# Attention, gated FFN and a mixture of experts in one kernel: the norm's weight beside the root, Newton on VectorE, masks zeroed by VectorE, a new order

## Chip, cores and metric

One Trainium2 chip; the kernel runs on one of its cores. The metric is device microseconds (us) of one execution, lower is better. Engines: PE is TensorE (matmuls), PEld its weight loads, DVE is VectorE, ACT ScalarE, POOL GpSimd, SP SyncE (it issues DMAs).

## What is computed

Three stages, one after the other, all float32. The heads of the attention's output lie side by side, so that 4 x 576 tokens of 8 x 64 features become x, 2304 x 512.

```python
# attention: batch 4, heads 8, seq 576, head_dim 64, window 64
scores = q @ k.T / 8 ; keep 0 <= i - j < 64 ; softmax ; @ v
# FFN: w_gate, w_val 512 x 1536, w_out 1536 x 512
rms = sqrt(mean(x*x, -1) + 1e-6);  xn = x / rms * rms_g
x = (silu(xn @ w_gate) * (xn @ w_val)) @ w_out
# experts: 8, w1 512 x 1024, w2 1024 x 512
e = argmax(x @ w_gate);  gate_w = softmax(...)[e];  eom = sigmoid(x @ w_output_gate)[e]
out = gate_w * eom * (relu(x @ w1[e]) @ w2[e])
```

## The kernel before

**Precision.** Nearly every matmul is run on pairs: an operand is rounded to fp32r ("hi", a cast, helper `hi_i`, L348 on ACT, L350 on POOL, L352 on DVE) and the rest is kept as a second fp32r ("lo", a subtraction, `lo_i`, L355). Three matmuls (hi hi, hi lo, lo hi) make a product. So each operand costs a cast and a subtraction, and ACT, DVE and POOL are kept busy beside PE. `times` is a TENSOR_TENSOR multiply (L358).

**Attention.** 18 tiles of 128 tokens. For the tiles below K["qzt"] the queries lie in a buffer q_all that is padded with zeros (`zeros`, L557), and the scores are 128x128 matmuls (L672 to L674) with the mask added by a matmul of `masks` against the identity (L661) for the first tiles. Later tiles run scores as 64-row matmuls on halves of the array (L700, called tiled here), 12 for a half tile, and add the mask on DVE. Then row maximum (L726, DVE), exponent (L730, ACT), reciprocal (L742), division (L747 on ACT, L358 on POOL or DVE), transposition (L763) and the product with the values into a bank, from where x is copied.

**Norm.** For each tile: squares, a matmul that sums them, mean (L869), a seed for 1/sqrt (L874, an exponent on the bits), two Newton steps on a column of 128 numbers (`newton`: ten chained operations, on POOL), a transposition on PE that spreads the root (L900), and `norm` (L906): four DVE instructions, each x times rms_g times root for 128 features. Then hi and lo of xn.

**FFN.** 12 chunks f of 128 hidden features, for groups of tiles: GROUPS puts units 0 and 1 (tiles 0 to 3) into group 0. L1050 to L1052 are the gate and value matmuls, L1062 to L1075 the activation, L1092 to L1094 the product with w_out. The FFN's weights arrive as 64-bit floats and are converted during group 0 (`conv`): c1 and c0 on ACT (L948, L953), then bit operations on DVE (L958, L969), then hi and lo. Chunks below K["lact"] take c0 on ACT, the rest a DVE operation in its place.

**Experts.** Tokens are routed, scattered to slots in HBM by indirect DMA, and worked through in blocks of up to 512 tokens: a "first" block during the last FFN group, a narrow block of 128 (L1547 to L1559), then wide ones (L1588 to L1590, L1622 to L1624). Results go out by an indirect DMA that POOL issues (`put`, L1640); each put waits until the one before it has landed. Weights are split into hi (cast) and lo (subtraction) as they come.

**What sets the order.** `Plan.order` is a list scheduler in Python that runs when the kernel is built. Each `pl.op` names the engines that may do it with a cost in us for each, buffers read and written, and a priority; the scheduler simulates five engines, a lock for operations of DVE and POOL ("pv"), buffers and DMAs, and writes every engine's instructions in the order that the simulation gives. K holds its tuned numbers. While PE has nothing ready near the start, it gets filler matmuls (L505), until K["warm"] us of the simulated time. So a changed cost moves instructions everywhere.

Of the kernel before, what the change touches and what calls it, by code (L numbers as in the profile page):

```python
# [32 lines left out]
HOP = 0.2  # L33
TICK, FULL = 3.4133, 1.275
HOPS = {"t": 0.0, "a": 0.12, "v": 0.12, "p": 0.12, "s": 0.0}
K = dict(
    qzt=6, spe=4, lact=12, warm=50, wf=1.17, flead=37.337, pvt=5, nwv=0, port=1, t0=44.466, pp=93.644,
    lead=1.877, clead=14.32, stag=6.769, stage=1.089, slack=0.045, mpe=5, nt=2, look=-0.002, marg=0.239, dw=2.625, ewl=20.108,
    ews=5.63, xld=30.179, xtn=3.067, mlead=8, vb=0.61, vb2=0.298, tb=124.917, share=-0.071, rlead=4.252, span=0.82, wl=3.695,
# [17 lines left out]
class Op:  # L57
    __slots__ = ("engs", "fn", "prio", "seq", "succ", "need", "deps", "bufs", "eng", "start", "end", "dma", "done", "dur", "rows", "lock")
# [9 lines left out]
class Plan:  # L68
# [10 lines left out]
    def op(self, engs, fn, r=(), w=(), hold=(), prio=0.0, dma=0.0, after=(), rows=1.0, lock="p"):  # L79
        o = Op()  # L80
        o.engs, o.fn, o.prio, o.seq, o.dma, o.rows = engs, fn, prio, len(self.ops), dma, rows
        o.lock = lock
# [33 lines left out]
    def order(self):  # L116
# [11 lines left out]
        def enable(o):  # L128
            for e in o.engs:
                t = max((d.end + (HOPS[e] if d.eng == e and not d.dma else HOP) for d in o.deps), default=0.0)  # L130
                heapq.heappush(wait, (t, o.seq, e, o))
# [6 lines left out]
        ticks = {}  # L138

# [29 lines left out]
        while left:  # L169
# [5 lines left out]
            for e in free:  # L175
# [3 lines left out]
                while ready[e]:  # L179
                    it = heapq.heappop(ready[e])  # L180
# [33 lines left out]
                    if e == "t":  # L214
                        c = pe_time(now, c, o.rows)
# [13 lines left out]
                    for b in o.bufs:  # L229
                        b.left -= 1  # L230
                        b.end = max(b.end, o.end)
                        if not b.left:
                            b.slot["buf"], b.slot["free"] = None, b.end + HOP
# [37 lines left out]
def attention_ffn_moe(  # L271
# [102 lines left out]
    def cost(n, kind):  # L374
        f = n / 512.0
        return {
            "hs": {"a": 0.12 + 0.48 * f, "p": 0.1 + 0.52 * f, "v": 0.09 + 0.29 * f},
            "ls": {"v": 0.09 + 0.555 * f, "p": 0.17 + 1.12 * f},
            "hp": {"a": 0.1 + 0.48 * f, "v": 0.08 + 0.56 * f},
            "lp": {"v": 0.08 + 0.56 * f},  # L380
        }[kind]
# [20 lines left out]
    def c_ident(e):  # L402
        t = ident.t
        nc.gpsimd.memset(t, 0.0)
# [4 lines left out]
    def c_masks(e):  # L409


        nc.gpsimd.memset(masks.t, 0.0)
# [24 lines left out]
    pl.op({"p": 0.4}, c_ident, w=[ident], prio=-100)  # L437
    pl.op({"p": 2.5}, c_masks, w=[masks], prio=-99)
# [115 lines left out]
    def zeros(e):  # L554
        for j in range(2):
            a = qz[64 * j:64 * j + 64, :, :, :, 64 - 64 * j:P - 64 * j].rearrange("p z i c t -> p (z i c) t")
            nc.gpsimd.memset(a.bitcast(F32), 0.0)  # L557

    if K["qzt"]:
        pl.op({"p": 1.9}, zeros, w=[(qb, "zeros")], prio=-99.5)  # L560

    def attention_front(t):
# [13 lines left out]
        if t < K["qzt"]:  # L576
            for j in range(2):
# [3 lines left out]
                def turned(j=j):  # L581
# [7 lines left out]
                    {"v": 0.6}, lambda e, own=own, turned=turned: scaled_lo(e, own(1), turned(), own(0)),  # L589
                    r=[rq, (qb, (j, 0))], w=[(qb, (j, 1))], prio=pr, lock="pv",  # L590
                )
        else:
# [4 lines left out]
                {"v": 0.6}, lambda e: scaled_lo(e, qb.t[:, 1], view(rq), qb.t[:, 0]), r=[rq, (qb, 0)], w=[(qb, 1)],  # L597
# [4 lines left out]
        if t == 0:  # L602
# [4 lines left out]
            pl.op({"v": 0.55, "p": 0.7}, kz, w=[(kt, "p")], prio=pr)  # L607
# [19 lines left out]
    def attention_tile(t, kt, rv):  # L627
# [8 lines left out]
        if t == 0:  # L636
            of = val[-1] = Buf("val")
            pl.op(
                {"p": 0.9, "v": 1.07},
# [7 lines left out]
            {"v": 0.62, "a": 0.97, "p": 1.1}, lambda e: hi_i(e, of.t[0:64], al.t[0:64]), r=[al], w=[of], prio=pv_, lock="pv"  # L647
# [3 lines left out]
        for hf in range(2):  # L651
# [3 lines left out]
            if zt:  # L655
                bk = bank()

                def mmz(e, bk=bk, hf=hf):
# [18 lines left out]
                    {"t": 1.36 + 0.2 * pm}, mmz, r=[qb, kt] + ([ident_b, masks] if pm else []), w=[bk], hold=[s],  # L677
# [13 lines left out]
            if not zt:  # L691
# [13 lines left out]
                pl.op({"t": 1.0}, mm, r=[qb, kt], w=bks, hold=[s], prio=ps_, rows=0.75)  # L705
                for j, bk in enumerate(bks):
# [12 lines left out]
                    pl.op({"v": 0.67}, mask, r=[bk, masks], w=[(s, j)], prio=ps_)  # L719
# [31 lines left out]
            pl.op({"v": 0.64}, mx, r=[sc or s], w=[mb], prio=ps_)  # L751
            pl.op({"a": 1.5}, ex, r=[sc or s, mb], w=[s, mb], prio=ps_)
            pl.op({"v": 0.15, "a": 0.17}, guard, r=[mb], w=[mb], prio=ps_)
            pl.op({"v": 0.15}, rc, r=[mb], w=[mb], prio=ps_)
            pl.op({"p": 1.08, "v": 0.64, "a": 1.2}, nm, r=[s, mb], w=[s], prio=ps_, lock="pv")
# [23 lines left out]
        for hf in range(2):  # L779
            px_ = pr + (4 + hf) * sg  # L780
            if t < K["pvt"]:
# [16 lines left out]
                for r in range(2):  # L798
# [4 lines left out]
                    pl.op({"a": 0.34, "v": 0.36}, ev3, r=[bk], w=[(x, (hf, r))], prio=px_)  # L803
                continue
            for r in range(2):
# [40 lines left out]
        pl.op({"a": 0.6, "v": 0.64, "p": 1.28}, sqr, r=[x], w=[sq], prio=pn_, lock="pv")  # L846
# [12 lines left out]
        if t >= K["spe"]:  # L859
            n = 1  # L860
            pl.op({"p": 1.21, "v": 0.66}, add, r=[sq], w=[sq], prio=pn_, lock="pv")
# [16 lines left out]
        def newton(e):  # L878
            ms, yy, a, b = (y.t[:, z:z + 1] for z in range(4))
            ne = ve[e]  # L880
            times(e, a, yy, yy)
            times(e, a, a, ms)
            ne.tensor_scalar(out=a, in0=a, scalar1=-0.5, scalar2=1.5, op0=ALU.mult, op1=ALU.add)
            times(e, yy, yy, a)
            times(e, a, yy, yy)
            times(e, a, a, ms)
            ne.tensor_scalar(out=b, in0=a, scalar1=0.375, scalar2=-1.25, op0=ALU.mult, op1=ALU.add)
            times(e, b, b, a)
            ne.tensor_scalar(out=b, in0=b, scalar1=1.875, scalar2=None, op0=ALU.add)
            times(e, yy, yy, b)  # L890

        pl.op({"a": 0.14, "v": 0.12}, mean, r=[bk], w=[y], prio=pn_)
        pl.op({"a": 0.25}, seed, r=[y, seed_b], w=[y], prio=pn_)
        pl.op({"p": 3.6, "v": 1.9} if t < K["nwv"] else {"p": 3.6}, newton, r=[y], w=[y], prio=pn_, lock="")
# [16 lines left out]
        pl.op({"v": 1.15}, norm, r=[x, bk2, g_sb], w=[x], prio=pn_)  # L911
# [13 lines left out]
    def conv(kind, f):  # L925
# [112 lines left out]
    def ffn_step(p, f, n, new, acc, pr):  # L1038
# [7 lines left out]
        def gv(e, w, bk, which):  # L1046
# [53 lines left out]
    def ffn_end(p, acc, pr):  # L1100
        for j in range(SIZES[p]):
# [13 lines left out]
            pl.op({"a": 0.58, "v": 0.64}, ev, r=[acc[j]], w=[(x2[p, j], 0)], prio=pr + 1)  # L1115
# [33 lines left out]
    def route(p):  # L1149
# [4 lines left out]
        for j in range(PT):  # L1154
# [21 lines left out]
            pl.op({"a": 0.6, "v": 0.65}, r2, r=[bk], w=[bx], prio=pr)  # L1176
# [33 lines left out]
        def rf(e):  # L1210
# [9 lines left out]
            {"v": 1.41}, rb, r=[g["lm"], iota_m] + ([rt_b["pf"][(p - 1) % 2]] if p else []),  # L1220
# [594 lines left out]
```

## Time and profile before

| what | value |
|---|---|
| median of 3 runs | 883.3 us (882.4 to 884.68) |
| the profiled execution | 887.55 us, span 885.5 us |
| PE busy | 855.3 us, 97% of the span, 5786 matmuls |
| DVE, ACT, POOL busy | 548.3, 400.5, 298.9 us |
| mean granted PE clock | 0.981 |

The span is the profiled part of the execution; 2.05 us lie outside of it. The profile gives busy time by engine, groups of instructions, waits (an engine's idle time and the instruction that ended it) and a timeline. PEclk is the clock that PE was granted, as a share of 2.4 GHz; 0.50 is the lower level, 1.2 GHz. A busy PE at that level does half as much.

### The profile page before, as it was taken

To read this page: it belongs to the slowest core of one execution; us is meant where nothing else is said; L and a number is where in the kernel's file an instruction comes from. 1 tells how busy PE (TensorE), PEld (TensorE's weight loads), DVE (VectorE), ACT (ScalarE), POOL (GpSimd) and SP (SyncE) were. 2 spreads that over 40 slices of the span, in tenths; PEclk is the share of its full clock that TensorE was granted. 3 is DMA by queue.
4 is the path that set the end of the run, shared out by engine and by line. 5 is a ranking of instruction groups with operands and counts; after the bars stand their busy time and mean duration, and the time that the engine had idled before them with its cause. 6 is when DMAs were issued, how large, how long until landed. Compare 5 with 4: busy or idle time off the path is not lost. (4 is left out here: it accounts for less than half of the span.)

```text
span 885.5 us, 16016 instructions
## 1 busy us (share of the span) xinstructions
PE 855.3 (97%) x5786; PEld 780.3 (88%) x5786; DVE 548.3 (62%) x1258; ACT 400.5 (45%) x1050; POOL 298.9 (34%) x510
## 2 busy tenths in 40 slices
PE   8989999999999999999999999999989999999995
PEld 8978998999899999889998999999968888989984
DVE  6887898977775673756466553554576253556640
ACT  7888776664643452445342342222333132343420
POOL 6886543315324231443224220210133132233320
PEclk8998999999999999999999999999998999999998
DMA  6266799637524431265014317540095344656500
GB/s 195 92 246 219 245 277 316 236 120 253 188 80 140 174 131 38 96 201 172 8 67 160 143 49 285 171 175 1 27 321 206 119 144 147 210 176 228 192 25 19
DMA packets 54016, 139.28 MB, mean 157 GB/s; under 512 B 6800, under 2 KB 6800, under 8 KB 53936
## 3 DMA queue, kind: packets, MB, share of 16 engines
q1 hardware_dynamic: 50912, 128.40, 42.9%
q0 software_dynamic: 3024, 9.85, 2.9%
q8 instruction: 46, 0.75, 0.4%
q14 instruction: 34, 0.28, 0.1%
HBM read 113.69 MB, written 24.54 MB: 156 GB/s over the span
## 5 line engine op out<-in xcount | busy, mean ns | idle before, releaser
L1050 PE MATMUL bank<-xn,w 128*128 128x384 f32 (+1 forms) x672 | 216.6, 322 | 3.3 <-POOL xn L350 2.3
L1051 PE MATMUL bank<-xn,w 128*128 128x384 f32 (+1 forms) x672 | 211.4, 315 | 0.6 <-DVE xn L355 0.6
L1052 PE MATMUL bank<-xn,w 128*128 128x384 f32 (+1 forms) x672 | 211.6, 315 | 0.2 <-DVE w L355 0.2
L1050 PEld LDWEIGHTS bank<-xn,w 128*128 128x128 f32 x672 | 128.1, 191 | 8.2 <-POOL xn L350 2.5
L1051 PEld LDWEIGHTS bank<-xn,w 128*128 128x128 f32 x672 | 128.2, 191 | 2.9 <-DVE xn L355 0.8
L1052 PEld LDWEIGHTS bank<-xn,w 128*128 128x128 f32 x672 | 128.0, 190 | 0.4 <-DVE w L355 0.4
L355 DVE TENSOR_TENSOR w<-raw,w 128x512 fp32r<-128x512 f32 x114 | 85.3, 790 | 10.7 <-POOL w L350 5.7
L1092 PE MATMUL bank<-wo,h 128*128 128x512 f32 x216 | 87.4, 405 | 1.3 <-POOL h L350 1.1
L1094 PE MATMUL bank<-wo,h 128*128 128x512 f32 x216 | 85.2, 394 | 0.0
L1093 PE MATMUL bank<-wo,h 128*128 128x512 f32 x216 | 85.0, 394 | 0.0
L1075 DVE TENSOR_TENSOR u<-u,bank 128x384 f32<-128x384 f32 (+1 forms) x84 | 41.5, 494 | 69.1 <-PE bank L1052 67.1
L1062 ACT ACTIVATE u<-bank 128x384 f32<-128x384 f32 (+1 forms) x84 | 37.2, 443 | 84.2 <-PE bank L1052 74.8
L350 POOL TENSOR_SCALAR w<-raw 128x512 fp32r<-128x512 f32 x59 | 36.3, 631 | 107.0 <-PE bank L1052 39.1
L1622 PE MATMUL bank<-w,eh 128*128 128x512 f32 (+1 forms) x168 | 67.9, 404 | 3.4 <-DVE eh L355 3.4
L1588 PE MATMUL bank<-xT,w 128*128 128x256 f32 (+4 forms) x224 | 68.5, 306 | 0.3 <-DVE eh L1599 0.3
L348 ACT CAST h<-u 128x384 fp32r<-128x384 f32 (+1 forms) x68 | 31.9, 470 | 80.2 <-DVE u L1075 74.1
L1590 PE MATMUL bank<-xT,w 128*128 128x256 f32 (+4 forms) x224 | 68.2, 304 | 0.0
L1589 PE MATMUL bank<-xT,w 128*128 128x256 f32 (+4 forms) x224 | 68.1, 304 | 0.0
L1067 DVE SCALAR_TENSOR_TENSOR u<-u,bank 128x384 f32<-128x384 f32 (+1 forms) x84 | 41.4, 493 | 42.1 <-ACT u L1062 41.5
L1624 PE MATMUL bank<-w,eh 128*128 128x512 f32 (+1 forms) x168 | 67.2, 400 | 0.0
L1623 PE MATMUL bank<-w,eh 128*128 128x512 f32 (+1 forms) x168 | 67.1, 400 | 0.0
L348 ACT CAST w<-raw 128x512 fp32r<-128x512 f32 x67 | 38.9, 618 | 35.1 <-PE bank L1052 17.4
(262 smaller groups left out, 1856.3 us busy)
## 6 DMA issues: line engine op xcount, KB each, us to landing
w<-whd SPq DMA_DIRECT2D x80, 512.0 KB, 3.8
raw<-in_moe_w_dram SPq DMA_DIRECT2D x64, 512.0 KB, 4.6
whd<-w SPq DMA_DIRECT2D x24, 512.0 KB, 5.1
raw<-in_moe_w_gate_dram SPq DMA_DIRECT2D x12, 512.0 KB, 5.4
raw<-in_moe_w_val_dram SPq DMA_DIRECT2D x12, 512.0 KB, 4.3
raw<-in_moe_w_out_dram SPq DMA_DIRECT2D x12, 512.0 KB
rx<-in_q_dram SPq DMA_DIRECT2D x18, 256.0 KB, 3.1
rx<-in_k_dram SPq DMA_DIRECT2D x18, 256.0 KB, 2.8
```

Of the source, the lines that this page charges most:

```text
L348: nc.scalar.copy(o, i)
L355: ve[e].tensor_tensor(out=o, in0=i, in1=h, op=ALU.subtract)
L1050: nc.tensor.matmul(o, lhsT=h_, rhs=xn.t[:, 0, kk], start=(kk == 0), stop=False)
L1051: nc.tensor.matmul(o, lhsT=h_, rhs=xn.t[:, 1, kk], start=False, stop=False)
L1052: nc.tensor.matmul(o, lhsT=l_, rhs=xn.t[:, 0, kk], start=False, stop=(kk == KD - 1))
L1092: nc.tensor.matmul(o, lhsT=h.t[:, 0, c], rhs=wo.t[:, 0, f], start=(n == 0), stop=False)
L1093: nc.tensor.matmul(o, lhsT=h.t[:, 0, c], rhs=wo.t[:, 1, f], start=False, stop=False)
L1094: nc.tensor.matmul(o, lhsT=h.t[:, 1, c], rhs=wo.t[:, 0, f], start=False, stop=(n == NF - 1))
L1588: nc.tensor.matmul(o, lhsT=wh, rhs=x.t[:, 0, kk, 0:N], start=(kk == 0), stop=False)
L1589: nc.tensor.matmul(o, lhsT=wh, rhs=x.t[:, 1, kk, 0:N], start=False, stop=False)
L1590: nc.tensor.matmul(o, lhsT=wl, rhs=x.t[:, 0, kk, 0:N], start=False, stop=(kk == KD - 1))
L1622: nc.tensor.matmul(bk.t[0:M], lhsT=hh, rhs=wh, start=(f == 0), stop=False)
```

## The change

- `masks` and `ident` are zeroed by DVE (`c_zero`); POOL only runs the selects on them. The zeros of q_all are two operations that either engine may take.
- A new operation `weigh` multiplies x by rms_g between the squares and the norm. `norm` becomes a single DVE instruction over 512 features.
- `newton` takes 8 instructions on DVE (10 on POOL, as before). It may go to either; the order gives 17 of 18 tiles to DVE. `weigh` went to ACT (four instructions) for all but one tile, which POOL has.
- Tiled scores of both halves of a tile get the same priority, and the scheduler charges 0.165 us for each change between tiled and other matmuls. K["qzt"] 7: tile 6 now has padded scores.
- K["lact"] 8: for the chunks from 8 on, c0 is replaced by a DVE operation.
- Costs of nearly all operations, a latency for each engine in place of one for all, and K are new, so the order is new. Instructions in the whole program: POOL 533 to 318, DVE 1286 to 1399, ACT 929 to 1036. Casts of the experts' weights: DVE 2 to 49, POOL 59 to 8; their subtractions on POOL 14 to 34. Fillers 182 to 250.

```diff
-HOP = 0.2
+SW = 0.165
-HOPS = {"t": 0.0, "a": 0.12, "v": 0.12, "p": 0.12, "s": 0.0}
+LAT = {"t": 0.17, "a": 0.15, "v": 0.15, "p": 0.12, "s": 0.2}
-    qzt=6, spe=4, lact=12, warm=50, wf=1.17, flead=37.337, pvt=5, nwv=0, port=1, t0=44.466, pp=93.644,
+    qzt=7, spe=4, lact=8, warm=60, wf=1.17, flead=36.084, pvt=5, nwv=1, port=1, t0=50.832, pp=94.912,
...
-        nc.gpsimd.memset(t, 0.0)
...
-        nc.gpsimd.memset(masks.t, 0.0)
...
+    def c_zero(e):
+        nc.vector.memset(ident.t, 0.0)
+        nc.vector.memset(masks.t, 0.0)
...
-                pl.op({"t": 1.0}, mm, r=[qb, kt], w=bks, hold=[s], prio=ps_, rows=0.75)
+                pl.op({"t": 0.67}, mm, r=[qb, kt], w=bks, hold=[s], prio=pr + 2 * sg + hf * K["hfs"], rows=0.75, tiled=True)
...
+        def weigh(e):
+            if e == "a":
+                for kk in range(KD):
+                    nc.scalar.activation(out=x.t[:, kk], in_=x.t[:, kk], func=AF.Copy, scale=g_sb.t[:, kk:kk + 1])
+            else:
+                both(e, x.t, x.t, g_sb.t.unsqueeze(2).to_broadcast([P, KD, P]), ALU.mult)
+
+        pl.op({"a": 1.05, "p": 1.3, "v": 0.64}, weigh, r=[x, g_sb], w=[x], prio=pn_ + 0.05, lock="pv")
...
-            times(e, a, yy, yy)
-            times(e, a, a, ms)
-            ne.tensor_scalar(out=a, in0=a, scalar1=-0.5, scalar2=1.5, op0=ALU.mult, op1=ALU.add)
-            times(e, yy, yy, a)
-            times(e, a, yy, yy)
-            times(e, a, a, ms)
-            ne.tensor_scalar(out=b, in0=a, scalar1=0.375, scalar2=-1.25, op0=ALU.mult, op1=ALU.add)
-            times(e, b, b, a)
-            ne.tensor_scalar(out=b, in0=b, scalar1=1.875, scalar2=None, op0=ALU.add)
-            times(e, yy, yy, b)
...
+            for c1, c0 in ((-0.5, 1.5), (0.375, -1.25)):
+                if e == "v":
+                    ne.scalar_tensor_tensor(out=a, in0=yy, scalar=yy, in1=ms, op0=ALU.mult, op1=ALU.mult)
+                else:
+                    times(e, a, yy, yy)
+                    times(e, a, a, ms)
+                ne.tensor_scalar(out=b, in0=a, scalar1=c1, scalar2=c0, op0=ALU.mult, op1=ALU.add)
+                if c1 > 0:
+                    times(e, b, b, a)
+                    ne.tensor_scalar(out=b, in0=b, scalar1=1.875, scalar2=None, op0=ALU.add)
+                times(e, yy, yy, b)
...
-        pl.op({"p": 3.6, "v": 1.9} if t < K["nwv"] else {"p": 3.6}, newton, r=[y], w=[y], prio=pn_, lock="")
+        pl.op({"v": 1.5} if t < K["nwv"] else {"p": 2.95, "v": 1.5}, newton, r=[y], w=[y], prio=pn_, lock="pv")
...
-            for kk in range(KD):
-                nc.vector.scalar_tensor_tensor(
-                    out=x.t[:, kk], in0=x.t[:, kk], scalar=g_sb.t[:, kk:kk + 1], in1=bk2.t[:, 0:P],
-                    op0=ALU.mult, op1=ALU.mult,
-                )
...
+            both("v", x.t, x.t, bk2.t[:, 0:P].unsqueeze(1).to_broadcast([P, KD, P]), ALU.mult)
```

**POOL at the start, before.** POOL's instructions up to the first select on the masks (an AFFINE_SELECT writes the value outside of a triangle):

```order
L404 MEMSET ident 128x128
L405 ISA
L405 AFFINE_SELECT ident<-ident 128x128
L557 MEMSET q_all 64x16x64 x2
L412 MEMSET masks 128x512
L416 AFFINE_SELECT masks<-masks 64x2x64
```

After the change, the same stretch of POOL:

```order
L569 MEMSET q_all 64x16x64
L414 ISA
L414 AFFINE_SELECT ident<-ident 128x128
L424 AFFINE_SELECT masks<-masks 64x2x64
L428 AFFINE_SELECT masks<-masks 64x2x64
```

One half of the zeros of q_all and the zeros of `ident` and `masks` left POOL; on DVE they are its first instructions and its seventh.

**Tile 3's root and norm, before.** POOL, from the Newton steps (y is the column with mean and root) to the cast of xn:

```order
L358 TENSOR_TENSOR y_1190<-y_1190 128x1 x2
L883 TENSOR_SCALAR y_1190<-y_1190 128x1
L358 TENSOR_TENSOR y_1190<-y_1190 128x1 x3
L887 TENSOR_SCALAR y_1190<-y_1190 128x1
L358 TENSOR_TENSOR y_1190<-y_1190 128x1
L889 TENSOR_SCALAR y_1190<-y_1190 128x1
L358 TENSOR_TENSOR y_1190<-y_1190 128x1
L350 TENSOR_SCALAR wo<-t_1219 128x512
L367 TENSOR_SCALAR q_all<-rx_839 64x8x64
L350 TENSOR_SCALAR xn<-x_1071 128x4x128
```

After the change, DVE for the same tile (L368 is `times`, and the norm where a bank is read; L977 and L988 convert weights):

```order
L905 SCALAR_TENSOR_TENSOR y_1262<-y_1262 128x1
L909 TENSOR_SCALAR y_1262<-y_1262 128x1
L368 TENSOR_TENSOR y_1262<-y_1262 128x1
...
L912 TENSOR_SCALAR y_1262<-y_1262 128x1
L368 TENSOR_TENSOR y_1262<-y_1262 128x1
L977 SCALAR_TENSOR_TENSOR t_1320<-t2k_1319,t_1320 128x512
L368 TENSOR_TENSOR x_1044<-x_1044,bank_1347 128x512
L988 SCALAR_TENSOR_TENSOR t_1320<-raw_1161,t_1320 128x512
L365 TENSOR_TENSOR xn<-x_1044,xn 128x4x128
```

The chain stands on DVE, with one weight operation between it and the norm, which is one row, and one between the norm and the lo of xn.

**The narrow expert block, before.** DVE around the lo of eh, the hidden layer of the narrow block (w are weights of the next expert):

```order
L355 TENSOR_TENSOR xT_8276<-bank_8297,xT_8276 128x4x64
L355 TENSOR_TENSOR w_8335<-raw_8230,w_8335 128x512
L355 TENSOR_TENSOR w_8337<-raw_8239,w_8337 128x512
L355 TENSOR_TENSOR w_8335<-raw_8230,w_8335 128x512
L355 TENSOR_TENSOR eh_8346<-bank_8345,eh_8346 128x512
```

After the change:

```order
L1532 COPY meta_3_154<-xs_8347 64x1
L362 CAST w_8390<-raw_8352 128x512 x2
L365 TENSOR_TENSOR eh_8376<-bank_8375,eh_8376 128x512
L365 TENSOR_TENSOR xT_8317<-bank_8382,xT_8317 128x4x128
L365 TENSOR_TENSOR eh_8393<-bank_8392,eh_8393 128x512
```

Three subtractions that need POOL's casts stood ahead of eh's lo; now two casts of DVE's own do, and the subtractions of that weight are POOL's.

## Rows read from the trace of the kernel before

**Rows 1.** Stretches: length; PE, PEld, DVE, ACT, POOL busy; PEclk, DMA, GB/s.

```profile
60.00:80.00 20.00, 16.04 (x106) 14.41 (x106) 18.73 (x35) 17.65 (x51) 12.88 (x19) 0.83 0.70 245
...
100.00:180.00 80.00, 78.27 (x586) 72.38 (x586) 73.96 (x139) 58.32 (x140) 31.34 (x38) 1.00 0.83 270
...
640.00:672.00 32.00, 26.99 (x118) 21.14 (x117) 22.54 (x63) 9.95 (x19) 9.40 (x13) 0.89 0.86 300
672.00:868.00 196.00, 195.68 (x1132) 172.48 (x1131) 100.24 (x189) 66.23 (x133) 61.05 (x74) 1.00 0.44 152
```

**Rows 2.** PE's waits: line and releaser, us in total, times, longest.

```profile
PE bank L900 <- POOL y L358: 3.5, 4, 1.5
PE bank L1622 <- DVE eh L355: 3.4, 1, 3.4
PE bank L1050 <- POOL xn L350: 2.3, 1, 2.3
PE bank L661 <- POOL masks L423: 2.1, 1, 2.1
```

**Rows 3.** A shorter stretch at the start, columns as in rows 1.

```profile
10.00:15.00 5.00, 5.00 (x32) 4.91 (x32) 2.69 (x7) 3.01 (x14) 1.47 (x3) 0.50 0.48 184
```

**Rows 4.** Timeline at the start, POOL: start, us, instruction.

```profile
1.32 1.94 POOL L557 MEMSET q_all<- 64x1024 f32 x2
3.32 0.53 POOL L412 MEMSET masks<- 128x512 bf16 x1
```

**Rows 5.** The same for PE.

```profile
8.11 0.38 PE L661 MATMUL bank<-masks,ident_b 128*128 128x512 bf16 x1 [2.08 <-POOL masks L423]
...
8.38 0.28 PE L673 MATMUL bank<-kt,q_all 128*128 128x128 f32 x1
8.49 0.30 PE L674 MATMUL bank<-kt,q_all 128*128 128x128 f32 x1
```

**Rows 6.** Timeline of POOL in tile 1's Newton steps.

```profile
43.25 1.25 POOL L358 TENSOR_TENSOR y<-y 128x1 f32<-128x1 f32 x2
...
48.23 0.19 POOL L358 TENSOR_TENSOR y<-y 128x1 f32<-128x1 f32 x1
```

**Rows 7.** Groups of DVE, 0 to 200 us: busy, mean ns, idle before.

```profile
L906 DVE SCALAR_TENSOR_TENSOR x<-x,g_sb,bank 128x128 f32<-128x128 f32 x24 | 6.7, 342 | 4.1 <-PE bank L900 4.1
...
L739 DVE TENSOR_SCALAR m<-m 128x4 f32<-128x4 f32 x4 | 2.5, 617 | 1.2 <-ACT s L730 1.2
...
L358 DVE TENSOR_TENSOR s<-s,m 128x512 f32<-128x512 f32 x2 | 1.4, 684 | 0.0
```

**Rows 8.** Timeline of DVE in the routing: chained small operations.

```profile
632.81 0.18 DVE L1184 TENSOR_TENSOR lm<-lg,mx 128x24 f32<-128x24 f32 x1
633.02 0.18 DVE L1188 SCALAR_TENSOR_TENSOR cd<-lm,iota_m 128x24 f32<-128x24 f32 x1
```

**Rows 9.** A group of ACT, whole span.

```profile
L747 ACT ACTIVATE s<-s,m 128x128 f32<-128x128 f32 x36 | 11.4, 393 | 0.6 <-DVE m L742 0.4
```

**Rows 10.** Timeline of PE around tiled scores.

```profile
152.83 0.91 PE L700 MATMUL bank<-kt,q_all 64*128 64x192 f32 x12
153.68 0.50 PE L1092 MATMUL bank<-wo,h 128*128 128x512 f32 x1
...
253.79 1.58 PE L700 MATMUL bank<-kt,q_all 64*128 64x192 f32 x24
255.31 0.44 PE L1050 MATMUL bank<-xn,w 128*128 128x384 f32 x1
```

**Rows 11.** Timeline of POOL, DVE and PE around the narrow expert block.

```profile
657.93 0.97 POOL L1640 DMA_INDIRECT out_dram<-osb,meta  x1 [8.02 <-ACT osb L1553]
...
659.60 4.53 DVE L355 TENSOR_TENSOR w<-raw,w 128x512 fp32r<-128x512 f32 x3 [4.11 <-POOL w L350]
664.05 0.68 DVE L355 TENSOR_TENSOR eh<-bank,eh 128x512 fp32r<-128x512 f32 x1
...
664.78 0.80 PE L1622 MATMUL bank<-w,eh 128*128 128x512 f32 x1 [3.40 <-DVE eh L355]
```

More of the change, by code (lines that the diff above doesn't have):

```diff
@@ L57 @@
 class Op:
-    __slots__ = ("engs", "fn", "prio", "seq", "succ", "need", "deps", "bufs", "eng", "start", "end", "dma", "done", "dur", "rows", "lock")
+    __slots__ = ("engs", "fn", "prio", "seq", "succ", "need", "deps", "bufs", "eng", "start", "end", "dma", "done", "dur", "rows", "lock", "tiled")
 class Filler:
@@ L77, in tag, with op @@
         self.tags[name] = [dict(make=m, gate=g, buf=None, free=0.0) for m, g in slots]
-    def op(self, engs, fn, r=(), w=(), hold=(), prio=0.0, dma=0.0, after=(), rows=1.0, lock="p"):
+    def op(self, engs, fn, r=(), w=(), hold=(), prio=0.0, dma=0.0, after=(), rows=1.0, lock="p", tiled=False):
         o = Op()
         o.engs, o.fn, o.prio, o.seq, o.dma, o.rows = engs, fn, prio, len(self.ops), dma, rows
-        o.lock = lock
+        o.lock, o.tiled = lock, tiled
         o.succ, o.deps, o.bufs, o.eng, o.done = [], set(after), [], None, False
@@ L129, in enable @@
             for e in o.engs:
-                t = max((d.end + (HOPS[e] if d.eng == e and not d.dma else HOP) for d in o.deps), default=0.0)
+                t = max((d.end + (0.0 if d.eng == e == "t" else LAT["s" if d.dma else d.eng]) for d in o.deps), default=0.0)
                 heapq.heappush(wait, (t, o.seq, e, o))
@@ L138, in order @@
         ticks = {}
+        tiled = False
         def pe_time(at, c, rows):
@@ L178, in order @@
                 skip = []
-                while ready[e]:
-                    it = heapq.heappop(ready[e])
+                first = None
+                if e == "t" and tiled and K["stk"]:
+                    first = min((x for x in ready[e] if x[2].tiled and not x[2].done), default=None)
+                    if first is not None and first[0] < min(x[0] for x in ready[e]) + K["stk"]:
+                        ready[e].remove(first)
+                        heapq.heapify(ready[e])
+                    else:
+                        first = None
+                while ready[e] or first is not None:
+                    it, first = (heapq.heappop(ready[e]), None) if first is None else (first, None)
                     o = it[2]
@@ L214, in order @@
                     if e == "t":
-                        c = pe_time(now, c, o.rows)
+                        c = pe_time(now, c + SW * (o.tiled != tiled), o.rows)
+                        tiled = o.tiled
                     o.dur = c
@@ L232, in order @@
                         if not b.left:
-                            b.slot["buf"], b.slot["free"] = None, b.end + HOP
+                            b.slot["buf"], b.slot["free"] = None, b.end + 0.13
                     for x in o.succ:
@@ L676, in attention_tile @@
                 pl.op(
-                    {"t": 1.36 + 0.2 * pm}, mmz, r=[qb, kt] + ([ident_b, masks] if pm else []), w=[bk], hold=[s],
+                    {"t": 1.33 + 0.2 * pm}, mmz, r=[qb, kt] + ([ident_b, masks] if pm else []), w=[bk], hold=[s],
                     prio=ps_,
@@ L717, in mask @@
                             )
-                    pl.op({"v": 0.67}, mask, r=[bk, masks], w=[(s, j)], prio=ps_)
+                    pl.op({"v": 0.88}, mask, r=[bk, masks], w=[(s, j)], prio=ps_)
             mb = Buf("m")
```

92 lines of the change are left out of this document (47 added, 45 removed).

## The prediction

> **What bounds the kernel now.** I read first how busy PE is by stretch of the span [rows 1]. From 672 to 868 us it works 195.68 of 196 us at full clock, and from 100 to 180 us 78.27 of 80: there nothing is to be had but fewer matmuls. It loses time in two places. From 60 to 80 us it works 16.04 of 20 us, and its clock is 0.83: the granted clock has the levels 1.0 and 0.5 (2.4 and 1.2 GHz), so a mean of 0.83 is 0.34 x 20 = 6.8 us at half speed, which cost 3.4 us of work. From 640 to 672 us it stands for 5.0 us, and 0.89 over 32 us is 7.0 us at half, worth 3.5 us.
>
> Next, whom PE waits for [rows 2]. The four entries hold 11.3 us: four waits for the root of the norm (POOL's Newton steps), one for the narrow expert block's eh, one for xn behind the last root of group 0, one for the masks. Third, a stretch at the start [rows 3]: from 10 to 15 us, with no wait, PE runs at 0.50, so 2.5 us of work are lost. In all three places the order is the same: PE stands, then its clock is low, then it comes back. A wait that goes may take its low clock along.
>
> Fourth, the other engines beside these waits [rows 1]: from 60 to 80 us DVE is busy 18.73 of 20 us and ACT 17.65, from 100 to 180 us DVE 73.96 of 80. The start and group 0 are a contest of four engines, and what PE doesn't wait for on POOL it may wait for on DVE.
>
> **The change part by part.** The profiled execution took 887.55 us, 885.5 of it span and 2.05 around it. It lies 4.25 above the median of 883.3. I sum against 887.55.
>
> *Masks.* POOL zeroed q_all in 1.94 us and the masks in 0.53 before the selects [rows 4]. One half of the first (0.97) and all of the second leave: 1.5 us. PE's first score stood 2.08 us for the masks, starting at 8.11 [rows 5]. The gain is between 0 (keys or queries are ready only then) and 2.1; I take -1.5, the row on POOL's path. DVE does these zeros as its first instructions and idles there, its inputs not having landed.
>
> *The clock behind it.* The half clock from 10 to 15 us [rows 3] costs 2.5 us of PE work. PE gets 68 more fillers, and the first scores follow sooner, so the clock may hold; what then counts is only what the softmax chain waits for. Between 0 and -2.5; I take -1, near the middle.
>
> *Newton and norm.* On POOL tile 1's chain runs from 43.25 to 48.42 us, 5.2 us for ten operations on a column [rows 6]. On DVE the change issues 8 per tile. DVE's chained small operations start 0.21 us apart [rows 8], which makes 1.7 us. A small DVE operation beside a busy POOL is seen at 0.617 us in the mean [rows 7], which makes 4.9: these are the ends. I take 1.7, since the chain leaves POOL less to do. The norm was four instructions of 0.342 (1.37 us), and becomes one over 512 features: a DVE multiply of that size took 0.684 [rows 7]. So DVE gains 1.7 + 0.7 - 1.4 = 1.0 us of work per tile. The multiplication by the weight goes to ACT, four activations of 128 x 128 at 0.393 [rows 9]: 1.6 us per tile, beside the sum and Newton, so it is hidden unless ACT is late with the mean and seed, which stand behind it on its queue. Four tiles in group 0: DVE +4, ACT +6.3, POOL up to four times 5.2 less.
>
> What it can give: the waits for roots and for xn, 3.5 + 2.3 [rows 2], and the 3.4 us that the low clock cost from 60 to 80 us, together 9.2. What takes it back: in that stretch DVE had 1.3 us free and ACT 2.35 [rows 1], and both get more. Also twelve conversions (chunks 8 to 11) move an operation from ACT to DVE, at most 0.684 each: up to +8 on DVE until about 100 us, and as much off ACT. I take -1.5 of the 9.2: the chain gets shorter, but DVE's queue, with one weight operation ahead of the norm and one ahead of xn's lo, is what the chain then waits in. Ends: -9.2, and a loss priced with the rivals.
>
> *The narrow expert block.* PE stands 3.40 us until 664.78 for the lo of eh [rows 11]. It was DVE's turn only at 664.05, since three subtractions stood ahead of it, and these had waited 4.11 us for casts that POOL runs behind a put that started at 657.93 [rows 11]. In the new order the subtractions of that weight are POOL's, and behind them on DVE nothing waits; ahead of eh's lo stand two casts that are DVE's own. So the lo comes as soon as its bank is done and the cast is made. Some 0.7 us for that lo itself may stay (0.68 us, [rows 11]). The gain is 3.4 - 0.7 = 2.7, and the low clock behind it, 3.5 at most, of which I take 2.3, since a short wait is left. Together -5; ends 0 (a DMA of the weight is late and the casts wait for it) and -6.9.
>
> *Tiled scores.* A block of 12 lasts 0.85 us to the next matmul, one of 24 lasts 1.52 [rows 10]: twelve more cost 0.67, so each block pays 0.18 for its way out. The new order has 14 blocks, the old one 20: -1.1, or twice that if the way in costs as much. Tile 6 goes over to padded scores: 24 matmuls 0.11 apart [rows 5] are 2.6 for 1.5 of tiled ones, +1.1. Four mask matmuls fewer, at 0.27 less 0.11 each [rows 5]: -0.6. Together -0.6 to -1.7; I take -1.
>
> *Experts' weights.* DVE gets 47 more casts (below 0.684 us each) and gives 20 subtractions of 0.684 to POOL: at most +18 us. From 672 to 868 us DVE is busy 100.24 of 196 us, POOL 61.05 [rows 1]. Both hide under PE. I cost it at nothing; if a put keeps POOL, a subtraction behind it comes late.
>
> **Sum:** -1.5 - 1 - 1.5 - 5 - 1 = -10: 887.55 becomes 877.5, and the median 873.3. Since the profiled execution was the slower one, and may have waited longer in just these places than the runs that made the median, I give back 0.7: **874**.
>
> **The rivals.**
>
> *DVE becomes the bound of group 0: slower.* Place: DVE's queue from 20 to 180 us. It gets 1.0 us per tile (8 tiles until 180 us), up to 8 for the conversions, and four masks that were matmuls, 0.684 each: up to 19 us. From 60 to 80 us it had 1.3 us free, from 100 to 180 us 6.0 [rows 1]. If no more of its stalls go than that, some 9 us arrive at PE as waits, and 3.4 us as another stretch at half clock; the start, the expert block and the tiled scores give back 8.5. That is +4: 887. It decides from the point where DVE's load passes its free time plus what POOL's absence from the shared memory path frees. For it: DVE's 73.96 of 80. Against it: POOL's small operations, up to four times 5.2 us, no longer stretch DVE's. The Trainium skill (SBUF — State Buffer, on its two separate sides) says that a DVE instruction with two operands in SBUF and a GpSimd instruction exclude each other for a whole instruction. The row of 0.617 us for a small operation agrees with that in direction; by that rule the Newton chain on DVE would stop at whatever POOL runs, and this rival would get more likely, with Newton at 4.9 us a tile. Chance 0.16.
>
> *The expert block doesn't gain.* The casts of DVE wait for a weight's DMA (the DMA engines are at 0.86 there [rows 1]), and eh's lo stands behind them as it stood behind the subtractions. Then -5 is missing: 879. For it: casts on DVE now stand where they wait for a landing. Against it: they read a weight that was to be cast earlier by POOL anyway. Chance 0.17.
>
> *It comes out even.* Group 0 loses about what the expert block gains: +5 for half of the first rival, -6 for the rest: 882 to 884. Chance 0.14.
>
> *Group 0 gains in full.* Both its waits and its low clock go, 9.2 in place of 1.5: 866. For it: the chain of POOL is the releaser of every one of these waits. Against it: DVE and ACT at 94% and 88% there [rows 1]. Chance 0.05.
>
> **How the numbers follow.** My forecast has 0.48. A change of this kernel under 0.3% (2.65 us) can't be told from none. Faster than 880.6 are the forecast, the expert block without gain, and group 0 in full: 0.48 + 0.17 + 0.05 = 0.70. Even is 0.14, slower 0.16. The range goes from 866 (the full gain of group 0) to 886, just short of the slower case, with one in ten beyond it and less below. The forecast's own range is 869 to 878.
>
> **What would show it.** Right: PE's first score near 6.6 us in place of 8.11; no wait for POOL at the spreading of the root; Newton on DVE 1.7 us a tile; the wait of 2.3 us for xn gone; the wait before the first product with the narrow block's eh under 1 us, and a mean clock above 0.89 from 640 to 672 us. Wrong: waits for DVE's root or xn of more than 6 us in all until 180 us, with DVE above 95% there; an eh that waits for DVE's casts; or a clock that falls anyway, without a wait.

## The result, and the profile after

The changed kernel takes 891.44 us, the median of 4 runs (889.95 to 892.17); the kernel before, with one more run, 882.92. The ratio is 1.0091 (95% interval 1.0070 to 1.0111): slower by 0.9%, 8.5 us, where 874 was forecast. The profiled execution of the changed kernel took 890.9 us with a span of 889.2, near its median; that of the kernel before lay above its own, so the two profiles differ by less (3.7 us of span) than the medians do.

The waits of PE after the change (line and releaser, us in total, times, longest), to be held against [rows 2]:

```profile
PE bank L687 <- DVE q_all L382: 4.8, 2, 4.0
PE bank L923 <- DVE y L368: 4.1, 3, 3.4
PE bank L923 <- DVE m L755: 2.2, 1, 2.2
...
PE bank L1641 <- DVE eh L365: 0.2, 1, 0.2
```

The waits for the masks and for xn are gone, and eh's is down to 0.2 us. A new one of 4.0 us for q_all heads the list. The root of the norm (L923), which POOL released before, is waited for longer than before, 6.3 us for 3.5, now from DVE (the 2.2 us entry too: that operation follows Newton's last one on DVE).

The stretches (length; PE, PEld, DVE, ACT, POOL busy; PEclk; DMA, GB/s), to be held against [rows 1]:

```profile
0.00:20.00 20.00, 16.47 (x169) 15.64 (x170) 14.38 (x32) 15.26 (x50) 12.07 (x44) 1.00 0.65 209
20.00:40.00 20.00, 14.79 (x192) 14.02 (x190) 18.54 (x29) 16.91 (x65) 13.00 (x14) 0.94 0.26 83
40.00:60.00 20.00, 19.53 (x164) 19.23 (x163) 13.57 (x31) 11.81 (x39) 5.61 (x7) 0.63 0.18 56
60.00:80.00 20.00, 14.46 (x146) 13.31 (x146) 17.14 (x36) 15.28 (x43) 8.40 (x9) 0.88 0.54 195
...
640.00:672.00 32.00, 30.02 (x172) 25.19 (x171) 20.97 (x89) 11.09 (x24) 8.89 (x10) 1.00 0.49 161
672.00:868.00 196.00, 194.56 (x1116) 170.27 (x1115) 122.61 (x218) 73.20 (x143) 62.22 (x50) 1.00 0.52 176
```

From 640 to 672 us PE works 30.02 us at full clock, where it was 26.99 at 0.89: the expected gain came, and more. From 0 to 20 us the clock is 1.00. But from 20 to 40 us PE is busy 14.79 of 20 us, and from 40 to 60 us it is busy 19.53 of 20 at a clock of 0.63, while DVE, ACT and POOL all have time to spare. This is the stretch to look at. From 672 us on, PE has more small gaps (194.56 us busy for 195.68), and DVE is busy 22 us longer.

Four places of PE's timeline (start, us, instruction) show where the kernel was ahead and where behind. After the change:

```profile
6.97 0.38 PE L674 MATMUL bank<-masks,ident_b 128*128 128x512 bf16 x1
...
79.74 0.47 PE L923 MATMUL bank<-ident,y 128*128 128x128 f32 x1 [3.37 <-DVE y L368]
...
669.07 0.50 PE L1641 MATMUL bank<-w,eh 128*128 128x512 f32 x1 [0.19 <-DVE eh L365]
```

And of the kernel before, tile 3's root:

```profile
65.00 0.32 PE L900 MATMUL bank<-ident,y 128*128 128x128 f32 x1 [0.96 <-POOL y L358]
```

The first score starts at 6.97 where it was 8.11 [rows 5], 1.1 us ahead. Tile 3's root is spread at 79.74, not 65.00: 14.7 us behind. The narrow block's second product starts at 669.07, not 664.78 [rows 11]: 4.3 behind. At the end it is 3.7. So the change wins some 10 us between 80 and 672 us, and it loses 16 us between the first score and tile 3's root. The orders differ, so one root is a rough mark (tile 4's is only 5.7 us behind); but the FFN's 145th gate or value matmul is late by as much, 16.6 us (it starts at 111.8, for 95.2).

**Where the 16 us arise.** DVE from 33 us on in the changed kernel:

```profile
33.04 0.69 DVE L365 TENSOR_TENSOR xn<-x,xn 128x512 fp32r<-128x512 f32 x1
33.76 5.62 DVE L382 SCALAR_TENSOR_TENSOR q_all<-rx,q_all 64x512 fp32r<-64x512 f32 x1
39.42 0.69 DVE L362 CAST p<-bank 128x512 fp32r<-128x512 f32 x1
```

POOL at the same time:

```profile
33.49 1.14 POOL L360 TENSOR_SCALAR val<-val 64x1024 fp32r<-64x1024 f32 x1 [3.75 <-PE bank L808]
34.60 0.61 POOL L360 TENSOR_SCALAR val<-rx 128x512 fp32r<-128x512 f32 x1
35.19 0.61 POOL L360 TENSOR_SCALAR w<-t 128x512 fp32r<-128x512 f32 x1
35.77 0.61 POOL L360 TENSOR_SCALAR kt<-kt 128x512 fp32r<-128x512 f32 x1
36.35 1.26 POOL L365 TENSOR_TENSOR val<-rx,val 128x512 fp32r<-128x512 f32 x1
37.58 1.26 POOL L365 TENSOR_TENSOR w<-t,w 128x512 fp32r<-128x512 f32 x1
```

And PE:

```profile
35.16 0.27 PE L686 MATMUL bank<-kt,q_all 128*128 128x128 f32 x1
39.44 0.47 PE L687 MATMUL bank<-kt,q_all 128*128 128x128 f32 x1 [4.01 <-DVE q_all L382]
```

A subtraction that DVE does in 0.65 us elsewhere takes 5.62. It begins 0.27 us after POOL has begun a run of six operations that follow each other without a break, and it ends 0.5 us after the last of them (38.84): its own time, once POOL is done. PE stands 4.0 us for it, and then its clock is low. Four stretches of 5 us:

```profile
35.00:40.00 5.00, 0.99 (x8) 0.85 (x6) 4.97 (x2) 3.37 (x10) 3.84 (x5) 0.76 0.00 0
40.00:45.00 5.00, 5.00 (x30) 5.00 (x30) 3.38 (x6) 0.76 (x3) 0.00 (x0) 0.50 0.30 105
45.00:50.00 5.00, 5.00 (x38) 5.00 (x37) 2.83 (x12) 3.51 (x13) 0.69 (x2) 0.50 0.00 0
50.00:55.00 5.00, 5.00 (x48) 4.88 (x47) 2.52 (x5) 2.96 (x6) 2.51 (x3) 0.54 0.00 0
```

Half clock from 40 us to nearly 55, with PE busy throughout: some 7 us of work lost behind a wait of 4. In these 15 us DVE, ACT and POOL are all busy far less than PE.

That POOL's operations follow each other isn't enough for such a stall. Earlier in the same profile DVE does the same kind of subtraction beside two casts of POOL (DVE's row first):

```profile
13.36 1.06 DVE L382 SCALAR_TENSOR_TENSOR q_all<-rx,q_all 64x512 fp32r<-64x512 f32 x1
```

```profile
13.28 0.62 POOL L360 TENSOR_SCALAR val<-rx 128x512 fp32r<-128x512 f32 x1
13.86 1.05 POOL L360 TENSOR_SCALAR kt<-kt 128x512 fp32r<-128x512 f32 x1
```

There is no gap between the casts either, but DVE ends 0.5 us after the first, and the second takes 1.05 us in place of 0.61: here DVE was let in between. The traces have many such places. Why it was let in there, and at none of the five places from 33.76 us on, no run shows.

### The profile page after: what moved, and what is told of

It is laid out like the page before. It is cut to its first block, busy times and chain, and to the rows that moved or that the text cites. A ratio compares the mean times of both kernels' runs of the same rounds, so it can differ in the third digit from the quotient of the medians.

```text
span 889.2 us, 16122 instructions
## 1 busy us (share of the span) xinstructions
PE 857.8 (96%) x5850; PEld 784.8 (88%) x5850; DVE 589.3 (66%) x1371; ACT 432.6 (49%) x1157; POOL 243.5 (27%) x295
## 4 chain that ended last, share of the span: by engine, by line
PE 78%; DVE 9%; issue 5%; ACT 3%; DMA 2%; POOL 1%; SPq 0%; POOLq 0%; ACTq 0%; DVEq 0%
PE bank L1069 11%; PE bank L1070 11%; PE bank L1071 11%; PE bank L1111 5%; PE bank L1113 5%; PE bank L1112 5%; PE bank L1641 3%; PE bank L1642 3%; PE bank L1643 3%; PE bank L832 3%; PE bank L1607 3%; PE bank L1608 2%; PE bank L1609 2%; DVE w L365 2%; PE bank L713 2%
## 5 line engine op out<-in xcount | busy, mean ns | idle before, releaser
L365 DVE TENSOR_TENSOR w<-raw,w 128x512 fp32r<-128x512 f32 x94 | 90.2, 987 | 0.7
L365 POOL TENSOR_TENSOR w<-raw,w 128x512 fp32r<-128x512 f32 x34 | 48.4, 1428 | 105.4 <-DVE w L362 69.2
L1641 PE MATMUL bank<-w,eh 128*128 128x512 f32 (+1 forms) x168 | 66.7, 397 | 0.2 <-DVE eh L365 0.2
L1643 PE MATMUL bank<-w,eh 128*128 128x512 f32 (+1 forms) x168 | 66.3, 394 | 0.0
L1642 PE MATMUL bank<-w,eh 128*128 128x512 f32 (+1 forms) x168 | 66.2, 394 | 0.0
L362 DVE CAST w<-raw 128x512 fp32r<-128x512 f32 x49 | 20.1, 444 | 59.6 <-PE bank L1643 32.0
```

Source lines behind the costliest of these rows:

```text
L365: ve[e].tensor_tensor(out=o, in0=i, in1=h, op=ALU.subtract)
L1641: nc.tensor.matmul(bk.t[0:M], lhsT=hh, rhs=wh, start=(f == 0), stop=False)
L1642: nc.tensor.matmul(bk.t[0:M], lhsT=hh, rhs=wl, start=False, stop=False)
L1643: nc.tensor.matmul(bk.t[0:M], lhsT=hl, rhs=wh, start=False, stop=(f == NF2 - 1))
```

## Experiments

Two theories for group 0. **P**: POOL's operations, one behind the other, keep a DVE instruction out; PE waits, and its clock falls. **L**: DVE and ACT simply have too much to do, Newton included (the rival of the forecast). The times of one kernel spread, the kernel before from 879 to 892 us in one round, so ratios are to it in the same runs. In each an order that the planner wrote is kept (the changed kernel's, unless the kernel before is named), and only what is said is changed in it. The code is shown in part, with "..." where lines are left out, and with comments that explain it.

**POOL waits for the subtraction.**

```diff
     # after the planner: 172 is DVE's subtraction of q_all, 131 POOL's first operation of the run
+    def then_mark(e, fn=at[172].fn):
+        fn(e)
+        nc.vector.memset(cell, 0.0)
...
+    def wait_mark(e, fn=at[131].fn):
+        nc.gpsimd.memset(cell, 0.0)
+        fn(e)
...
+    at[172].fn, at[131].fn = then_mark, wait_mark
```

Both write one cell, so POOL's write has to wait for DVE's, and with it POOL's run.

> The changed kernel, but POOL begins its run of six operations near 33.5 us only when DVE has done the second subtraction of q_all that stood 5.62 us in the changed kernel (one DVE and one POOL memset of a single cell, so that POOL waits for DVE). Theory P (POOL's operations, one behind the other, keep a DVE instruction with two SBUF operands out for the whole run; PE stands for it and its clock stays low behind it): the subtraction takes about 0.7 us, PE's wait of 4.0 us at 39.4 us is gone, the half clock from 37.6 to 54.6 us is gone or much shorter, and the time falls by 6 to 12 us against the changed kernel, to 880 to 885. Theory L (group 0 is bound by what DVE and ACT have to do, Newton's steps included; the stall is hidden in other waiting): the stall goes, but the end of group 0's attention comes at most 3 us earlier, and the time is 888 to 892.

882.75 us, ratio 0.9985 (0.9951 to 1.0018): all of the loss is gone. DVE and POOL, timeline:

```profile
34.66 0.69 DVE L382 SCALAR_TENSOR_TENSOR q_all<-rx,q_all 64x512 fp32r<-64x512 f32 x1
35.40 0.06 DVE L1787 MEMSET cell<- 1x1 f32 x1
```

```profile
35.52 0.09 POOL L1790 MEMSET cell<- 1x1 f32 x1 [4.50 <-DVE cell L1787]
35.58 1.04 POOL L360 TENSOR_SCALAR val<-val 64x1024 fp32r<-64x1024 f32 x1
```

```profile
40.00:45.00 5.00, 4.50 (x58) 4.13 (x58) 4.56 (x15) 4.94 (x16) 3.06 (x4) 1.00 0.15 52
```

The subtraction takes 0.69 us, PE's clock is 1.00 from 35 to 50 us (one stretch shown, columns as above), and the span is 9.1 us shorter (880.1). Nothing was taken from DVE's work: theory P, not L.

**Fillers in the gap: the wait or the clock?**

```diff
+GAP_T, GAP_H = 3, 0
...
+                            gap = (t, hf, i, c) == (GAP_T, GAP_H, 0, 0)
...
+                            if gap:
+                                for _ in range(28):    # each fill is two matmuls
+                                    fill("t")
                             nc.tensor.matmul(o[:, i, c], lhsT=ql, rhs=kh, ...
```

> The changed kernel with 56 filler matmuls (4.4 us at full clock) put into PE's queue ahead of the matmul that waits 4.0 us for q_all at 39.4 us; the wait itself stays. If the clock behind the wait is the larger part of the loss (theory P, second half): PE's clock stays at 1.0 from 37.6 to 54.6 us, and about 6 us of the loss in this stretch are gone: 884 to 887. If PE's clock costs nothing there because DVE, ACT and POOL set the pace (theory L): the clock may stay, the time does not change, 890 to 892.

887.87 us, a little above the 884 to 887 expected, ratio 1.0023 (0.9982 to 1.0064). The subtraction still takes 5.63 us, and the matmul that waits for it still starts at 39.17 us. The clock is another (two of the stretches of 5 us, columns as above):

```profile
40.00:45.00 5.00, 5.00 (x64) 5.00 (x64) 4.69 (x10) 3.21 (x14) 0.47 (x1) 1.00 0.35 105
45.00:50.00 5.00, 4.50 (x56) 4.02 (x55) 4.83 (x13) 4.94 (x12) 3.67 (x5) 1.00 0.01 3
```

The profiled execution has a span of 882.0, 7.2 us less than the changed kernel's, by matmuls that compute nothing. But it was the fastest of the ten executions, 4.2 us under their median. Of the 9 us that the stall cost, the clock behind it took 7 in the profiles, 6 by the ratios (1.0091 to 1.0023, and to 0.9985), and 4 by the medians (891.44 to 887.87, and to 882.75). So between 4 and 7.

**Newton back on POOL.**

```diff
+    for o in seq:
+        if o.fn.__name__ == "newton":
+            o.eng = "p"
```

> The changed kernel with the Newton steps of all tiles on POOL (ten operations each), everything else in the same order. Theory L (Newton in DVE's queue is what binds group 0): faster than the changed kernel by 4 us or more, 884 to 887. Theory P: Newton is not the cause; on POOL each takes 3 to 5 us in place of 1.7 to 3.7, the waits for the root grow, and the time is the same or up to 6 us longer, 891 to 897.

897.12 us, ratio 1.0126 (1.0065 to 1.0186), against 1.0091 for the changed kernel: the intervals overlap, the profile's span is 7.3 us longer (896.5). PE's waits, and a row of DVE:

```profile
PE bank L923 <- POOL y L368: 7.3, 7, 1.5
PE bank L687 <- DVE q_all L382: 5.7, 2, 4.9
```

```profile
34.17 5.72 DVE L365 TENSOR_TENSOR xn<-x,xn 128x512 fp32r<-128x512 f32 x1
```

DVE is rid of 136 small operations (8 for each of 17 tiles), and it doesn't get better. So L falls a second time; Newton on DVE is no loss in this order, and probably a gain. The stall came again, through the same six operations of POOL, but it hit another subtraction of DVE, xn's lo (34.17 us).

From 180 to 640 us PE was busy 456.71 us here and 459.55 in the changed kernel, so this order needs Newton on DVE there. The gain of the change in this stretch is not thereby Newton's. The kernel before, with Newton on POOL in an order made for that, was busy 455.71 us there, and among its waits of that stretch the root has 0.2 us:

```profile
PE bank L1233 <- DVE x L831: 1.7, 2, 1.4
PE bank L1092 <- POOL h L350: 1.1, 2, 0.6
...
PE bank L900 <- POOL y L358: 0.2, 1, 0.2
```

L1233 is a matmul of the routing. Which part of the new order took these waits away, no run shows.

**The experts' weights.**

```diff
+    for o in seq:                      # wts: the operations that split the experts' weights
+        if o.eng == "p" and getattr(o.fn, "wts", False):
+            o.eng = "v"
```

> The changed kernel with all splitting of the experts' weights that POOL did (34 subtractions, 8 casts) moved to DVE at the same place in the order; POOL keeps only the puts there. Theory X (the 3 us that the changed kernel loses from 672 us to the end come from POOL's 1.3 us subtractions standing in the way of DVE's): DVE's subtractions take 0.68 us again, PE's waits of 0.96 and 0.69 us in this stretch go, and the time falls by 2 to 4 us, to 887 to 889. Rival (the order of DVE's work in this stretch is what is late): DVE has 23 us more to do, the waits stay or grow, 891 to 894.

888.3 us, ratio 1.0029 (1.0004 to 1.0053). The groups of DVE's weight subtractions, changed kernel and this one (count, busy us, mean ns):

```profile
L365 DVE TENSOR_TENSOR w<-raw,w 128x512 fp32r<-128x512 f32 x94 | 90.2, 987 | 0.7
```

```profile
L365 DVE TENSOR_TENSOR w<-raw,w 128x512 fp32r<-128x512 f32 x128 | 83.7, 683 | 0.4 <-ACT w L358 0.2
```

The stretch of the experts in this kernel, columns as above:

```profile
672.00:868.00 196.00, 196.00 (x1139) 173.57 (x1138) 117.49 (x256) 75.46 (x146) 22.67 (x17) 1.00 0.52 177
```

And the start of the narrow block's second product, which stands at 669.07 in the changed kernel:

```profile
670.12 0.50 PE L1642 MATMUL bank<-w,eh 128*128 128x512 f32 x1
```

128 subtractions take DVE less time than 94 did, since POOL no longer does any beside them; PE is busy 196.00 of 196 us, and the span is 2.6 us shorter. From the narrow block's second product to the end it is 216.5 us for 220.1, 3.6 less. So POOL's help cost more than it gave.

**Both repairs, then Newton kept free too.**

```diff
 # both: the two edits above; then, for the second kernel, two more pairs of hold
...
+(161, 1006)   # POOL's subtraction of w waits for Newton of tile 2
+(210, 244)    # POOL's division of scores waits for Newton of tile 3
```

A pair (first, later) puts the write of a cell behind DVE's operation `first` and POOL's write of it ahead of POOL's `later`, as in the first run.

> The changed kernel with two repairs together: POOL's run near 33.5 us begins behind DVE's subtraction of q_all (as in the first run), and DVE does all splitting of the experts' weights that POOL did (as in the fourth). Both were worth 9 and 2.6 us of span alone, at places 600 us apart. If they are separate losses, as theory P says, they add up: a span near 877.5, 876 to 881 in time, and faster than the kernel before by about half a per cent. If the second only pays where DVE is late from the start, the time is that of the first repair alone, 882.

878.66 us, ratio 0.9937 (0.9896 to 0.9979): within this interval they add up.

> As the last, and POOL is also held back until DVE has done the Newton steps of tile 2 (before a subtraction of w of 1.27 us) and of tile 3 (before the division of scores). Theory P: Newton, stretched there from 1.7 to 3.6 us by POOL's operations between its small ones, takes 1.7 us, the waits for the root of 2.2 and 3.4 us shrink by up to 1.9 us each, a stretch at half clock may go with them: another 2 to 6 us, 872 to 879. Rival: what POOL is kept from is late then, or the root is late because its input is (ACT's mean and seed): no change against the last kernel.

873.63 us, ratio **0.9858** (0.9811 to 0.9905): 5 us better again by the medians (the intervals still touch), and 1.4% faster than the kernel before. In the changed kernel Newton of tile 3 ran from 76.07 to 79.69 us, and two of its rows were:

```profile
76.48 0.90 DVE L368 TENSOR_TENSOR y<-y 128x1 f32<-128x1 f32 x1
...
78.17 1.13 DVE L368 TENSOR_TENSOR y<-y 128x1 f32<-128x1 f32 x1
```

With POOL held back it runs from 64.17 to 65.76, first and last operation, and PE's root:

```profile
64.17 0.19 DVE L905 SCALAR_TENSOR_TENSOR y<-y 128x1 f32<-128x1 f32 x1
...
65.60 0.16 DVE L368 TENSOR_TENSOR y<-y 128x1 f32<-128x1 f32 x1
```

```profile
65.82 0.32 PE L923 MATMUL bank<-ident,y 128*128 128x128 f32 x1 [1.35 <-DVE cell L1793]
```

3.6 us become 1.6, and the root comes at 65.8. From 40 to 60 us PE's clock is 1.00 here (0.91 with the first repair alone), so another stretch at half clock went as well. The span is 4.0 us shorter than with the two repairs (870.7 for 874.7). With the 9.1 us of the first hold that makes 13 of the 16 us lost in group 0, and the FFN's 145th gate or value matmul starts at 98.1 again. The last 3 us stay open.

**Parts of the change in the old order.** The kernel before, Newton's place in its order kept, the operation on DVE; then also the norm.

```diff
 # kernel before, first of the two
+        if o.fn.__name__ == "newton":    # in the new form, 8 instructions
+            o.eng = "v"
 # second: also, behind the seed on ACT, and the norm in one instruction
+                nc.scalar.activation(out=x.t[:, kk], in_=x.t[:, kk], func=AF.Copy, scale=g_sb.t[:, kk:kk + 1])
+            both("v", x.t, x.t, bk2.t[:, 0:P].unsqueeze(1).to_broadcast([P, KD, P]), ALU.mult)
```

> The kernel before, its order kept, with the Newton steps of all tiles on DVE in the new 8 instructions; nothing else of the change. If Newton on DVE is good by itself, as the third run suggests (5 us worse without it): the waits for POOL's root (3.5 us) go, and the time falls by 2 to 6 us, 877 to 881. If the order must be made for it (in the old one DVE's queue stands still for the seed, and group 0 has 1 us more of DVE per tile): the same or slower, 883 to 889.

890.62 us, ratio 1.0055 (1.0028 to 1.0083): slower. Waits of PE:

```profile
PE bank L1051 <- POOL xn L350: 2.3, 1, 2.3
PE bank L1051 <- DVE u L1068: 2.0, 2, 1.2
PE bank L850 <- ACT xf L842: 1.9, 3, 1.1
PE bank L1095 <- DVE h L355: 1.8, 2, 1.2
```

No wait for the root is left, but now PE waits for the squares and longer for u and h; the wait for xn stays. That Newton stands in DVE's queue where the old order had not planned for it is the likely reason, and not shown.

> As the last, and the norm as in the change: the weight multiplied on ACT (four activations behind the seed), the norm one DVE instruction. DVE has 0.7 us less per tile than in the last kernel and ACT 1.3 us more. If the norm's DVE time lies on the chain of group 0: 1 to 3 us faster than the last. If ACT was as full there: no change.

887.09 us, ratio 1.0025 (0.9987 to 1.0063): perhaps 3 us better than the last, not to be told from the kernel before. So in the old order neither Newton alone nor both parts together show a gain.

**One break in POOL's run.** POOL may start the run, but waits before the second operation.

```diff
+(172, 176)    # 176: POOL's second operation of the run, the cast of the next val
```

> The changed kernel, where POOL may begin its run near 33.5 us with the first operation (a cast of val, 1.1 us), but begins the second only when DVE has done the subtraction of q_all: one break in the run, nothing else. If a DVE instruction gets in as soon as POOL's operations stop following each other without a break: the subtraction takes 1.0 to 1.8 us in place of 5.62 (what is left of the cast, and its own 0.65), and the time is within 2 us of the first run's 882. If POOL's first operation, a cast of 64 x 1024, is itself what keeps DVE out for long, the subtraction still takes more than 3 us, and the time is 887 to 892.

881.69 us, ratio 0.9998 (0.9959 to 1.0037). POOL's first cast and DVE's subtraction:

```profile
33.41 1.14 POOL L360 TENSOR_SCALAR val<-val 64x1024 fp32r<-64x1024 f32 x1 [3.75 <-PE bank L808]
```

```profile
33.69 1.41 DVE L382 SCALAR_TENSOR_TENSOR q_all<-rx,q_all 64x512 fp32r<-64x512 f32 x1
```

1.41 us: the rest of the cast under way and its own time. So it isn't that cast that costs 5 us, but the five others that follow it without a break.

**The changed kernel again, on that chip.**

> The changed kernel as it is, on the same chip as the last, since the kernel before spread from 879 to 895 us on the chips of the other runs. Theory P needs the 5.62 us stall and the half clock from 37 to 54 us in this run's profile too, and a time 7 to 10 us above the last kernel's. If the stall depends on chance (POOL and DVE arriving within tenths of a microsecond), it is gone in this profile and the time is near the last kernel's.

892.31 us, ratio 1.0118 (1.0068 to 1.0169). The profile has the subtraction at 33.93 with 5.62 us and PE's wait of 4.0 us. So it is not chance: the order brings POOL and DVE together there in every profile where it runs unheld. The time is 10.6 us above the kernel with the break.

## Why the prediction was wrong, step by step

- **Masks** (-1.5): right; 1.1 us came, 8.11 to 6.97 for the first score.
- **The clock behind it** (-1): under-sized. In this profile the clock is 1.00 to 37 us; 0.83 over the first 20 us before means 3.4 us. Some of the experiments' profiles had a half clock from 15 to 19 us, so not all of it is sure.
- **Newton and norm** (-1.5 net for group 0): **this step failed.** In its place group 0 lost 16 us, 9 of them by one stall. The sizes of Newton were right at their ends: 1.6 us on an undisturbed DVE, and 3.5 and 3.6 us for tiles 2 and 3 with POOL beside it, between the ends 1.7 and 4.9. The mistake was the direction in which the shared memory path was booked. I argued that POOL's small operations leaving it would free DVE, and charged DVE only its added work. But POOL's large casts and subtractions stayed, the new order ran six of them one behind the other, and a DVE instruction that met them, no part of the change itself, stood 5.62 us. Of the 9 us that this cost, 4 to 7 were PE's clock. Newton of tiles 2 and 3, stretched beside POOL, cost another 4 us of span. The gain to be had was booked too high as well: of the 3.5 us of waits for roots only 2.5 lay in group 0 (the others stand at 142.6 and 281.8 us).
- **The rival that DVE binds group 0** had the sign and, at 887, half of the loss, but not the mechanism. Its sum has a slip: 19 us of load less the 1.3 and 6.0 that were free are 11.7, not 9, so by its own rows it came to 890; that would have been near the time by luck. It priced DVE's load, and the run with POOL held back has the same load and none of the loss. The sign named for it came half true: PE waited 6.3 us for DVE's root until 180 us, but DVE was not above 95% (73.91 of 80 us from 100 to 180).
- **The rule on the shared path** was weighed in that rival as one that slows Newton, and not as one that can stop any instruction of DVE. The Trainium skill (SBUF — State Buffer, on its two separate sides) says that a DVE instruction with two operands in SBUF and a GpSimd instruction that reads SBUF exclude each other for a whole instruction. The subtraction of 1.41 us agrees with it: the rest of one cast, then its own time. The 5.62 us go further, since POOL's next instruction got in first five times running; elsewhere in the same trace DVE got in after one. The kernel before has a small case, a q_all subtraction of 2.50 us at 24.25 us that ended 0.5 us after the last of three operations of POOL. I read this row only after the result; ahead of it I had the mean of that group, 0.856 us, in which it can't be seen.
- **The narrow expert block** (-5): right, also in its mechanism. The wait went from 3.40 to 0.19 us, the clock stayed at 1.00, and from 640 to 672 us PE gained 3.0 us busy and some 3 by the clock, 6 in all.
- **Tiled scores** (-1): not measured apart. From 180 to 640 us PE gained 3.8 us busy, mostly waits for the routing and for h; no run tells which part of the change they belong to.
- **Experts' weights** (0): wrong by some 3 us. They don't hide: subtractions on POOL stretched DVE's from 683 to 987 ns, and PE got gaps. From the narrow block's second product to the end the kernel before took 220.7 us, with some 3 of them lost at half clock until 672 us; the changed one has full clock until 868 us and still takes 220.1.

The forecast's size, 874, is what the change does once POOL is held back in three places and the weights are DVE's (873.63). That is luck and no merit of the sum: it took for granted that nothing new would be in the way. The chances also didn't fit the range: the slower case had 0.16, but only one in ten was left above 886.

## What to carry to other kernels

When work is moved between VectorE and GpSimd, book not only the two loads but where in time both have operands in SBUF. The worst case of these runs was a row of six GpSimd instructions without a break; a hold that let VectorE go first delayed GpSimd's run by 2.1 us at most (35.58 us for 33.49) and gave back 9. A wait near the start can cost more than its length if PE's clock falls behind it: look at the clock in the stretches that follow. Idle matmuls in the gap gave back a part, and taking the wait away gave back all. A reordering that loses can hold a gain: find the one place where its plan and the chip part.

## What the runs showed of the hardware that I had not expected

- A DVE instruction with two SBUF operands waited through six GpSimd instructions, 5.62 us for 0.65 of work, in both profiles of the changed kernel and in two of its variants; in a third the same six held another instruction for 5.72. With one break in the run it was let in after the first (1.41 us).
- It isn't so wherever GpSimd runs without a break: at 13.36 us of the changed kernel the same kind of subtraction was let in between two casts that follow each other (1.06 us). What decides it is open.
- After a wait of 4 us PE ran 15 us at half clock while it was busy all the time; in a profile with 56 idle matmuls (3.3 us busy) in the wait it stayed at full clock.
- 94 subtractions on VectorE beside 34 on GpSimd took 90.2 us of VectorE; all 128 on VectorE took 83.7.
